# Four small moves in a one-core attention + MLP kernel: the q eviction of quad 1, the load of alpha, what delays the first casting transfers, and the PSUM tiles of one A@V

## The chip, the cores and the metric

The kernel runs on one core of a Trainium2 chip. The metric is the device time of one execution in microseconds; each version is run several times and its median is taken. A core has five engines that each work through their own list of instructions in order: TensorE (PE: matmuls, PEld: weight loads), VectorE (DVE), ScalarE (ACT), GpSimd (POOL) and SyncE (SP). They wait for each other through semaphores only. DMAs are issued from the lists of SP, ACT and POOL.

## The reference, cut to what matters

```python
def _attn_ref(q, k, v):                    # 8 batches, 12 heads, 448 positions, head size 64
    scores = scale * np.matmul(q, k.transpose(0, 1, 3, 2))
    attn = np.maximum(scores, 0.0) ** 2 / S
    return np.matmul(attn, v)

def _moe_ref(x, w_in, w_out, alpha):       # x: 3584 x 768, hidden size 2048
    h = x @ w_in
    g = np.maximum(h, 0.0) + alpha * np.minimum(h, 0.0)
    return g @ w_out
```

Attention without a softmax (relu, then squared) is followed by a two-layer MLP with a leaky relu whose slope alpha is given for each hidden unit. All inputs are float32; the kernel multiplies in bfloat16 and accumulates in float32.

## The kernel before, in words

**Tiling.** Four heads of one batch are a *quad*: two pairs (index r or s) of two heads (on the two halves of the 128 partitions). There are 3 quads in a batch (g = 0 to 2) and 24 in all. The 448 positions are 7 groups (j) of 64. For a unit (n, j), that is quad n and key group j, `scores` (L169) runs four 64x64 matmuls into a PSUM tile, then a relu writes it to SBUF as `rl`: "act" is one ACT instruction on 128x896 (L185), "both" one half on ACT (L163) and one on DVE (L165). `squares` (L188) multiplies two such units at a time by themselves on DVE (L196, 128x1792); its argument `keep` says how many finished units it may leave for later. `attnv` (L208) multiplies the seven squared units of a quad with v (28 matmuls, L223) and evicts the result, scaled, to `xT`. The MLP's first layer is `ffn1` (L248): 6 matmuls of 128x448 for each of the 16 blocks of 128 hidden units, over the six 128-row pieces km of the input (km // 2 is the quad g of the batch), then ACT writes the negative part (`neg`, L262) and DVE forms `gT` with beta = 1 - alpha (L263). The second layer is `ffn2` (L266).

**PSUM.** `sc_ps` (tag sc) has two buffers of two banks each, `mm_ps` (tag mm) four of one bank. A new tile in a pool waits for the readers of the tile that had the buffer before.

**Getting q, k and v in.** Of quad 0, q and k come as float32 on SP's queue (L357, L360: k in two pieces, groups 0 to 2 and 3 to 6) and are cast by ACT and DVE (L372, L373, L375, L378). Later quads of batches 0 and 1 come by DMAs that cast to bfloat16 on the way, issued by POOL (`load_bf16`, L93, and L367). PE transposes them to PSUM (`transpose`, L119, matmuls at L131), and DVE (L106) or ACT (L104) copies the result to `qT` and `kT`. From quad 6 on, other ways are used. The early casts live in `early_pool`, two buffers for each of q and k.

**Order.** The schedule is manual: each engine's list has its instructions in the order in which the program emits them. The start-up (L341 to L386) does quad 0's first units; the loop over n = 0 to 2 (L387 to L411) does the rest of batch 0's scores. Within it, at j = 3 the transposes and the eviction of k of quad n + 1 are emitted, at j = 4 those of q. After each unit, L398 calls `squares(keep=1)`; its condition `j != 4 or last or not 0` is always true:

```python
            elif j != 4 or last or not 0:
                squares(keep=1)
```

So at n = 0, j = 4 the square of units (0, 2) and (0, 3) stands in DVE's list ahead of the copy of quad 1's q. From the end of this loop on, MLP matmuls of one batch fill PE around the attention of the next.

**alpha.** It is 8 KB, loaded by ACT's queue first of all (L352). PE transposes it (L384) after the first scores, and DVE makes beta of it (L385). A one-column POOL copy from alpha into quad 1's k tile (L366) makes the first casting transfer (L367) wait until alpha has landed; the casts of quad 1's q, of v of quads 0 and 1 and so on follow it in POOL's list.

**The last A@V of batch 1.** `attnv(5)` (L471) takes one `sc_ps` tile for both halves, and one ACT instruction on 128x896 evicts it (L241). Around it stand `ffn1(1, 0)`, `ffn1(1, 1)` before, and `ffn1(1, 2)` behind, all with km = 0 to 3; then the matmuls with km = 4 and 5, which read what this eviction writes (L474, L475). `feed(7, "v")` (L472), a DVE cast, is emitted just after `attnv(5)`. With `apart=True`, which L422 uses for quad 2, an A@V takes two `sc_ps` tiles, and for later batches a list of two tiles is evicted by DVE (L238) and ACT (L239), a half each.

Of the kernel before, what the change touches and what calls it, by code (L numbers as in the profile page):

```python
# [11 lines left out]
BF16 = mybir.dt.bfloat16  # L12
# [8 lines left out]
NJ = 7  # L21
# [3 lines left out]
def kernel(  # L25
# [10 lines left out]
    nc = tc.nc  # L36
    B, H, S, D = q.shape
    d_model, d_ff = moe_w_in.shape
    assert H * D == d_model and S == PP * NJ and D == 64 and H % 4 == 0
    NG = H // 4  # L40
    n_pe = 2 * NG
    KM = d_model // 128
    KF = d_ff // 128
# [4 lines left out]
    def pool(name, bufs, **kw):  # L48
        return ctx.enter_context(tc.tile_pool(name=name, bufs=bufs, **kw))
# [6 lines left out]
    early_pool = pool("early", 2)  # L56
# [12 lines left out]
    alpha_sb = singles.tile([KF, 128], F32)  # L69
# [7 lines left out]
    raw, cast, qT, kT, vb = {}, {}, {}, {}, {}  # L77
    src = {"q": q, "k": k, "v": v}

    def flat(n, w):  # L80
        b, g = quads[n]
        return src[w][b, 4 * g:4 * g + 4].rearrange("(s hf) (pp j) d -> (hf pp) s (j d)", hf=2, j=NJ)

    def load(n, names="qkv", after=None):
        for w in names:
            t = raw_pool.tile([128, 2, NJ, D], F32, tag=w, name=f"{w}raw")
            raw[(n, w)] = t
            if after is not None:
                nc.gpsimd.tensor_copy(t[:, 0, 0, 0:1], after)
                after = None  # L90
            nc.sync.dma_start(out=t.rearrange("p s j d -> p s (j d)"), in_=flat(n, w))

    def load_bf16(n, names="kqv"):  # L93

        for w in names:
            if w == "v":
                t = vb[n] = v_pool.tile([128, 2, NJ, D], BF16, tag="v", name="vb")
            else:
                t = cast[(n, w)] = early_pool.tile([128, 2, NJ, D], BF16, tag=w, name=f"{w}e")
            nc.gpsimd.dma_start(out=t.rearrange("p s j d -> p s (j d)"), in_=flat(n, w))  # L100
# [7 lines left out]
    def to_bf16(n, w, eng):  # L108
        r = raw.pop((n, w))
        if w == "v":  # L110
            t = v_pool.tile([128, 2, NJ, D], BF16, tag="v", name="vb")
            vb[n] = t
            copy(eng, t, r)
        else:
            t = cast_pool.tile([128, NJ, 2, D], BF16, tag=w, name=f"{w}b")
            cast[(n, w)] = t
            copy(eng, t.rearrange("p j s d -> p s j d"), r)

    def transpose(n, w, js=range(NJ), eng=None):  # L119
        store = qT if w == "q" else kT  # L120
        if n not in store:
            store[n] = qkT_pool.tile([128, NJ, 2, PP], BF16, tag=w, name=f"{w}T")
        t, dst = cast[(n, w)], store[n]
        if n >= n_pe:
            nc.sync.dma_start_transpose(out=dst.rearrange("p j h c -> p j (h c)"),
                                        in_=t.rearrange("p j s d -> p (j s d)"))
            return
        ps = mm_ps.tile([128, NJ, 2 * PP], BF16, tag="mm", name="tps")
        for j in js:
            for s in range(2):  # L130
                nc.tensor.transpose(ps[64 * s:64 * s + 64, j], t[:, s, j], ident)  # L131
        lo, hi = js[0], js[-1] + 1
        copy(eng or nc.vector, dst[:, lo:hi].rearrange("p j h c -> p j (h c)"), ps[:, lo:hi])
# [74 lines left out]
    def attnv(n, js=range(NJ), space=sc_ps, apart=False):  # L208
        b, g = quads[n]
        if js[0] == 0:  # L210
            if space is mm_ps:
                av_ps[n] = [mm_ps.tile([128, 512], F32, tag="mm", name="avh") for _ in range(2)]
            elif apart:
                av_ps[n] = [sc_ps.tile([128, 2, 512], F32, tag="sc", name="av2")[:, 0] for _ in range(2)]
            else:
                av_ps[n] = sc_ps.tile([128, 2, 512], F32, tag="sc", name="av")
        ps = av_ps[n]
        half = ps if isinstance(ps, list) else [ps[:, r] for r in range(2)]
        for j in js:
            a = att.pop((n, j))  # L220
            for r in range(2):
                for s in range(2):
                    nc.tensor.matmul(half[r][64 * s:64 * s + 64, :S],  # L223
                                     vb[n][64 * r:64 * r + 64, s, j, :],
                                     a[64 * r:64 * r + 64, s],
                                     start=(j == 0), stop=(j == NJ - 1))
        if js[-1] != NJ - 1:
            return
        if g == 0:
            xT[b] = xT_pool.tile([128, NG, 2, S], BF16, tag="xT", name="xT")  # L230
        if b == 0:
            nc.scalar.activation(xT[b][:, g, 0], half[0][:, :S], ACTF.Copy, scale=out_scale)  # L232
            if g > 0:
                nc.vector.tensor_scalar(xT[b][:, g, 1], half[1][:, :S], out_scale, None, ALU.mult)
            else:
                nc.scalar.activation(xT[b][:, g, 1], half[1][:, :S], ACTF.Copy, scale=out_scale)
        elif isinstance(ps, list):
            nc.vector.tensor_scalar(xT[b][:, g, 0], half[0][:, :S], out_scale, None, ALU.mult)  # L238
            nc.scalar.activation(xT[b][:, g, 1], half[1][:, :S], ACTF.Copy, scale=out_scale)  # L239
        else:  # L240
            nc.scalar.activation(xT[b][:, g], ps[:, :, :S], ACTF.Copy, scale=out_scale)  # L241
# [69 lines left out]
    NQ = len(quads)  # L311
    def group(units, how="both"):

        def f():
            order = sorted(units, key=lambda u: u[1] == "av")
            for i, (n, j) in enumerate(order):
                if j == "av":
                    if (n, NJ - 1) not in att:
                        squares(single=nc.vector)
                    attnv(n)  # L320
                elif i == 0 and len(order) == 3:
                    scores(n, j, how, mm_ps)
                else:
                    scores(n, j)
            squares()
            for n, j in order:
                if n < n_pe:
                    continue
                if j == 0:
                    if n + 2 < NQ:  # L330
                        load(n + 2)
                    if n + 1 < NQ:
                        transpose(n + 1, "k")
                        transpose(n + 1, "q")
                if j == 4 and n > 2 * NG and n + 2 < NQ:
                    for w in "kqv":
                        to_bf16(n + 2, w, nc.gpsimd)
        return f


# [8 lines left out]
        for _ in range(count):  # L349
            nc.tensor.matmul(ps[:, 0, :256], warm_w, warm_x, start=True, stop=True)  # L350

    nc.scalar.dma_start(out=alpha_sb, in_=moe_alpha.rearrange("(kf p) -> kf p", p=128))  # L352
    for w in "qk":
        raw[(0, w)] = raw_pool.tile([128, 2, NJ, D], F32, tag=w, name=f"{w}raw")
        cast[(0, w)] = early_pool.tile([128, 2, NJ, D], BF16, tag=w, name=f"{w}e")
# [2 lines left out]
    for js in (first, rest):  # L358
        lo, hi = js[0], js[-1] + 1
        nc.sync.dma_start(out=raw[(0, "k")][:, :, lo:hi].rearrange("p s j d -> p s (j d)"),  # L360
                          in_=flat(0, "k")[:, :, lo * D:hi * D])
    make_identity(nc, ident)
    make_identity(nc, ident_f)

    cast[(1, "k")] = early_pool.tile([128, 2, NJ, D], BF16, tag="k", name="ke")
    nc.gpsimd.tensor_copy(cast[(1, "k")][:KF, 0, 0, 0:1], alpha_sb[:, 0:1])  # L366
    nc.gpsimd.dma_start(out=cast[(1, "k")].rearrange("p s j d -> p s (j d)"), in_=flat(1, "k"))  # L367
    load_bf16(1, "q")
    load_bf16(0, "v")
    load_bf16(1, "v")  # L370
    warm(15)
# [15 lines left out]
    for n in range(NG):  # L387
        last = n == NG - 1
        for j in range(NJ):
            if n == 0 and j < 3:  # L390
                continue
            if j == 2 or j == (4 if last else 5):
                scores(n, j, "both", mm_ps)
            else:
                scores(n, j, "act")
            if j == 6 and last:
                squares()
            elif j != 4 or last or not 0:  # L398
                squares(keep=1)
            if j == 3 and n > 0:  # L400
                attnv(n - 1, space=mm_ps)
            if j == 3 and not last:
                transpose(n + 1, "k")
            if j == 4 and not last:
                transpose(n + 1, "q")
                squares(keep=1)

            if last and j > 4:
                ffn1(0, j - 5, range(0, 4))
            if last and j == 6:  # L410
                ffn1(0, 2, range(0, 4))  # L411
        if n == 0:
            load_bf16(2)
            load_w_in(0, 512)
            load_w_in(512, 1024)
            load_w_in(1024, 2048)
            load_bf16(3)
# [41 lines left out]
    f = [fn for _, fn in steps(0, "in")]  # L459
# [8 lines left out]

    ffn1(1, 0, range(0, 4))
    ffn1(1, 1, range(0, 4))  # L470
    attnv(5)  # L471
    feed(7, "v")()  # L472
    ffn1(1, 2, range(0, 4))
    for ff in range(3):  # L474
# [107 lines left out]
```

## Time and profile before

| what | value |
|---|---|
| median of 4 runs | 391.56 us |
| lowest and highest run | 391.09 and 393.16 us |
| the profiled execution's own time | 391.09 us |
| its span, first to last instruction | 389.3 us |
| time around the span | 1.8 us |
| granted TensorE clock | 1.000 |
| busy: PE, DVE, ACT, POOL | 379.2, 252.6, 215.6, 74.0 us |

Times inside the profile count from the start of the span. A group line names the source line, the engine, the operation, and output <- input; in the timeline the first two numbers are the start and the length in us of one or several (xN) merged instructions, and the square bracket tells how long the engine had been idle before and what ended that. The chain of waits is the sequence of work that ended last, followed back from the end. Durations of matmuls overlap: in a dense stretch 96 matmuls of 128x448 take 18.16 us, 0.19 each, while the row of a single one says 0.35.

### The profile page before, as it was taken

The page shows a single profiled execution, that of the slowest core. Times are in us where ns is not written, and L with a number is a line of the kernel's source. Part 1 is how long each engine was busy: PE and PEld are TensorE (multiplying, and loading weights), DVE is VectorE, ACT ScalarE, POOL GpSimd, SP SyncE. Part 2 cuts the span into 40 slices and gives each one's busy share as a digit, 9 for nine tenths or more (in the row PEclk, how much of TensorE's full clock was granted, in tenths as well). Part 3 has the DMA queues.
Part 4 walks back from the last instruction along what each step waited for, and adds up shares of the span by engine and source line. Part 5 has one row for each costly group of instructions (what it writes and reads, how often), then busy time and mean ns, then how long its engine had stood idle before and what let it go on. Part 6 is the DMA issues. An engine that isn't in the chain of part 4 may idle for free.

```text
span 389.3 us, 7871 instructions
## 1 busy us (share of the span) xinstructions
PE 379.2 (97%) x3210; PEld 215.1 (55%) x3210; DVE 252.6 (65%) x335; ACT 215.6 (55%) x361; POOL 74.0 (19%) x88
## 2 busy tenths in 40 slices
PE   7699999999999999999999999999999999999996
PEld 4345556445665456645665455654566545655564
DVE  3976887687687767766675666777676376726411
ACT  5964768564566656664573645756565366624200
POOL 6654000052241113201231012311030000000000
PEclk9999999999999999999999999999999999999999
DMA  7999998995994619735494355947153220130033
GB/s 161 187 209 204 205 207 289 259 252 123 262 264 166 128 64 242 220 67 162 100 262 142 68 163 100 271 132 186 18 91 88 69 47 2 42 81 2 0 83 81
DMA packets 64755, 55.43 MB, mean 142 GB/s; under 512 B 35776, under 2 KB 60496, under 8 KB 64720
## 3 DMA queue, kind: packets, MB, share of 16 engines
q1 hardware_dynamic: 53472, 44.77, 45.2%
q0 software_dynamic: 10976, 9.96, 16.1%
q8 instruction: 25, 0.41, 0.4%
q10 hardware_dynamic: 272, 0.21, 0.2%
q14 instruction: 10, 0.08, 0.1%
HBM read 45.62 MB, written 11.01 MB: 145 GB/s over the span
## 4 chain that ended last, share of the span: by engine, by line
PE 93%; ACT 3%; DVE 1%; DMA 1%; issue 1%; ACTq 0%
PE hps L255 37%; PE ops L271 37%; PE avh L223 7%; PE sc L156 6%; PE sch L156 3%; ACT rl L185 2%; PE ops L294 1%; PE av L223 1%; PE tps L131 1%; DMA qraw<-in_q_dram 1%; DVE at L196 0%; ACT xT L232 0%; ACT xT L241 0%; ACT rl L163 0%; DVE gT L263 0%
## 5 line engine op out<-in xcount | busy, mean ns | idle before, releaser
L255 PE MATMUL hps<-xT,w_in_sb 128*128 128x448 bf16 x768 | 149.3, 353 | 0.8 <-ACT xT L232 0.4
L271 PE MATMUL ops<-w_out_sb,gT 128*128 128x384 bf16 x864 | 145.8, 326 | 0.1
L263 DVE SCALAR_TENSOR_TENSOR gT<-neg,beta_sb,hps 128x448 bf16<-128x448 f32 x128 | 85.6, 679 | 60.8 <-ACT neg L262 60.0
L271 PEld LDWEIGHTS <-gT 128*128 128x128 bf16 x864 | 83.5, 98 | 61.1 <-issue 7.9
L255 PEld LDWEIGHTS <-w_in_sb 128*128 128x128 bf16 x768 | 74.0, 98 | 72.8 <-issue 5.9
L262 ACT ACTIVATE neg<-hps 128x448 f32<-128x448 f32 x128 | 69.2, 546 | 63.7 <-PE hps L255 62.9
L185 ACT ACTIVATE rl<-sc 128x896 bf16<-128x896 f32 x87 | 77.4, 927 | 44.0 <-PE sc L156 44.0
L196 DVE TENSOR_TENSOR at<-rl 128x1792 bf16<-128x1792 bf16 x80 | 86.2, 1121 | 2.1 <-ACT rl L185 0.9
L106 DVE COPY osb<-ops 128x384 f32<-128x384 f32 x30 | 16.7, 557 | 45.7 <-PE ops L271 45.7
L163 ACT ACTIVATE rl<-sch 128x448 bf16<-128x448 f32 x81 | 41.7, 552 | 4.6 <-PE sch L156 4.6
L106 POOL CAST kb<-kraw 128x896 bf16<-128x896 f32 x16 | 18.7, 1166 | 114.1 <-DMA kT<-kb 56.7
L156 PE MATMUL sc<-qT,kT 64*64 64x448 bf16 x456 | 35.9, 355 | 4.1 <-ACT rl L185 1.4
L223 PE MATMUL avh<-at,vb 64*64 64x448 bf16 x588 | 34.2, 350 | 0.0
L156 PEld LDWEIGHTS <-kT 64*64 64x64 bf16 x672 | 21.9, 106 | 20.3 <-issue 12.8
L104 ACT COPY osb<-ops 128x384 f32<-128x384 f32 x24 | 11.4, 475 | 36.0 <-PE ops L271 36.0
L223 PEld LDWEIGHTS <-vb 64*64 64x64 bf16 x672 | 25.6, 106 | 9.3 <-issue 4.5
L183 DVE TENSOR_SCALAR rl<-sc 128x896 bf16<-128x896 f32 x27 | 29.4, 1090 | 0.6 <-PE sc L156 0.6
L106 POOL CAST vb<-vraw 128x896 bf16<-128x896 f32 x16 | 15.9, 992 | 36.3 <-PE avh L223 36.0
L106 POOL CAST qb<-qraw 128x896 bf16<-128x896 f32 x16 | 16.6, 1035 | 32.4 <-DMA qT<-qb 32.4
L156 PE MATMUL sch<-qT,kT 64*64 64x448 bf16 x216 | 22.5, 355 | 0.0
L165 DVE TENSOR_SCALAR rl<-sch 128x448 bf16<-128x448 f32 x27 | 16.8, 623 | 2.6 <-ACT xT L239 0.8
L238 DVE TENSOR_SCALAR xT<-avh 128x448 bf16<-128x448 f32 x19 | 11.9, 626 | 7.7 <-PE avh L223 7.7
(55 smaller groups left out, 97.7 us busy)
## 6 DMA issues: line engine op xcount, KB each, us to landing
out_dram<-osb SPq DMA_DIRECT2D x54, 192.0 KB, 2.8
qraw<-in_q_dram SPq DMA_DIRECT2D x19, 448.0 KB, 5.4
kraw<-in_k_dram SPq DMA_DIRECT2D x18, 448.0 KB, 4.4
vraw<-in_v_dram SPq DMA_DIRECT2D x18, 448.0 KB, 6.0
w_out_sb<-in_moe_w_out_dram POOLq DMA_DIRECT2D x2, 1536.0 KB, 20.1
w_in_sb<-in_moe_w_in_dram POOLq DMA_DIRECT2D x8, 192.0 KB, 8.5
w_in_sb<-in_moe_w_in_dram POOLq DMA_DIRECT2D x4, 384.0 KB, 10.0
vb<-in_v_dram POOLq DMA_DIRECT2D x6, 224.0 KB, 9.4
```

Source lines behind the costliest of these rows:

```text
L106: eng.tensor_copy(o, i)
L156: nc.tensor.matmul(half[r][64 * c:64 * c + 64, :S], kT[n][64 * r:64 * r + 64, j, c, :], qT[n][64 * r:64 * r + 64, :, c, :], start=True, st ...
L163: nc.scalar.activation(rl[:, r], half[r][:, :S], ACTF.Relu)
L165: nc.vector.tensor_scalar(rl[:, r], half[r][:, :S], 0.0, None, ALU.max)
L183: nc.vector.tensor_scalar(rl, ps[:, :, :S], 0.0, None, ALU.max)
L185: nc.scalar.activation(rl, ps[:, :, :S], ACTF.Relu)
L196: nc.vector.tensor_tensor(a, t, t, ALU.mult)
L223: nc.tensor.matmul(half[r][64 * s:64 * s + 64, :S], vb[n][64 * r:64 * r + 64, s, j, :], a[64 * r:64 * r + 64, s], start=(j == 0), stop=(j ...
L255: nc.tensor.matmul(ps, w_in_sb[:, km // 2, km % 2, bass.ts(ff, 128)], xT[b][:, km // 2, km % 2, :], start=(km == 0), stop=(km == KM - 1))
L262: nc.scalar.activation(neg, ps, ACTF.Relu, scale=-1.0)
L263: nc.vector.scalar_tensor_tensor(gT[b // 2][:, ff, (b % 2) * S:(b % 2) * S + S], neg, beta_sb[:, ff:ff + 1], ps, ALU.mult, ALU.add)
L271: nc.tensor.matmul(ps, gT[sb][:, ff, bass.ts(c, 128)], w_out_sb[:, ff, bass.ts(hf, 384)], start=(ff == 0), stop=(ff == KF - 1))
```

## The change

- **q of quad 1.** At n = 0, j = 4 the call of `squares` ahead of `transpose(1, "q")` is left out; the call behind it (unchanged) emits the same square. In DVE's list the copy of q of quad 1 and the square of units (0, 2), (0, 3) change places. Nothing else in the loop differs.
- **alpha.** Its DMA goes from the head of ACT's list to SP's, behind the three loads of quad 0.
- **Casting transfers.** POOL's one-column copy that waited for alpha is gone. Instead POOL fills quad 1's q tile and then its k tile with zeros (two memsets of 128x896 bfloat16), and the two transfers into them follow, k first as before.
- **A@V of quad 5.** It takes two `sc_ps` tiles and is evicted in two halves, by DVE (L238, 128x448) and ACT (L239, 128x448), where one ACT instruction did all of it. In DVE's list the new eviction stands ahead of the cast of v of quad 7.
- A stretch of `group` that no call reaches is removed; line numbers below it fall by up to 12.

```diff
@@ group
             squares()
-            for n, j in order:
-                if n < n_pe:
-                    continue
...
@@ start-up
-    nc.scalar.dma_start(out=alpha_sb, in_=moe_alpha.rearrange("(kf p) -> kf p", p=128))
     for w in "qk":
         raw[(0, w)] = raw_pool.tile([128, 2, NJ, D], F32, tag=w, name=f"{w}raw")
...
+    nc.sync.dma_start(out=alpha_sb, in_=moe_alpha.rearrange("(kf p) -> kf p", p=128))
     make_identity(nc, ident)
     make_identity(nc, ident_f)
 
-    cast[(1, "k")] = early_pool.tile([128, 2, NJ, D], BF16, tag="k", name="ke")
-    nc.gpsimd.tensor_copy(cast[(1, "k")][:KF, 0, 0, 0:1], alpha_sb[:, 0:1])
-    nc.gpsimd.dma_start(out=cast[(1, "k")].rearrange("p s j d -> p s (j d)"), in_=flat(1, "k"))
-    load_bf16(1, "q")
+    for w in "qk":
+        cast[(1, w)] = early_pool.tile([128, 2, NJ, D], BF16, tag=w, name=f"{w}e")
+        nc.gpsimd.memset(cast[(1, w)], 0.0)
+    for w in "kq":
+        nc.gpsimd.dma_start(out=cast[(1, w)].rearrange("p s j d -> p s (j d)"), in_=flat(1, w))
     load_bf16(0, "v")
@@ loop over batch 0
             if j == 6 and last:
                 squares()
-            elif j != 4 or last or not 0:
+            elif n > 0 or j != 4:
                 squares(keep=1)
@@ batch 1
-    attnv(5)
+    attnv(5, apart=True)
     feed(7, "v")()
```

More of the change, by code (lines that the diff above doesn't have):

```diff
@@ L325, in f @@
             squares()
-            for n, j in order:
-                if n < n_pe:
-                    continue
[L329 to L337, printed above, removed]
         return f
```

## The prediction, made before the changed kernel was run

> **What bounds the kernel now.** I read the chain of waits first, then the timeline where the chain leaves PE, then each engine's own timeline there, then the landings of the POOL transfers.
>
> The page's chain by engine and by line:
>
> ```profile
> PE 93%; ACT 3%; DVE 1%; DMA 1%; issue 1%; ACTq 0%
> ```
>
> 93% is PE, in an unbroken run of matmuls but for two places: the first 22 us and one eviction. Only there can the change win time; anywhere else it can only lose. The chain of the first 30 us, and of 68 to 78 us:
>
> ```profile
> 0.74 3.51 DMA qraw<-in_q_dram
> ...
> 10.14 1.00 DVE at L196
> 11.14 0.55 DVE qT L106
> ...
> 11.73 0.41 PE sc L156 x4
> ...
> 20.69 0.69 ACT xT L232
> ...
> 21.42 0.92 PE hps L255 x4
> ```
> ```profile
> 70.80 1.48 PE av L223 x28
> 72.28 0.02 issue
> 72.30 0.93 ACT xT L241
> 73.23 0.04 issue
> 73.27 3.00 PE hps L255 x15
> ```
>
> The first fence shows the square of (0, 2), (0, 3) and the q copy in series ahead of quad 1's scores; the second, one ACT eviction that PE waits for. PE and DVE in their own timelines of the start:
>
> ```profile
> 9.31 0.58 PE L131 MATMUL tps<-ident,qe 128*64 128x128 bf16 x14
> 11.73 0.57 PE L156 MATMUL sc<-qT,kT 64*64 64x448 bf16 x8 [1.34 <-DVE qT L106]
> 13.32 0.38 PE L223 MATMUL avh<-at,vb 64*64 64x448 bf16 x4
> ```
> ```profile
> 9.52 0.62 DVE L106 COPY kT<-tps 128x896 bf16<-128x896 bf16 x1
> 10.06 1.08 DVE L196 TENSOR_TENSOR at<-rl 128x1792 bf16<-128x1792 bf16 x1
> 11.06 0.62 DVE L106 COPY qT<-tps 128x896 bf16<-128x896 bf16 x1
> 11.59 0.61 DVE L165 TENSOR_SCALAR rl<-sch 128x448 bf16<-128x448 f32 x1
> 12.31 2.09 DVE L196 TENSOR_TENSOR at<-rl 128x1792 bf16<-128x1792 bf16 x2
> ...
> 21.18 0.62 DVE L234 TENSOR_SCALAR xT<-avh 128x448 bf16<-128x448 f32 x1
> ```
>
> What decides my forecast: from 8.52 to 24.87 DVE has no gap over 0.1 us. It is full, though the chain names ACT. PE's 1.34 us of idleness is thus not simply to be had.
>
> POOL's start, and the landing views of its first two transfers (last number: us from issue to landing):
>
> ```profile
> 1.43 0.19 POOL masks.py:199 TENSOR_SCALAR_AFFINE_SELECT ident_f<-ident_f 16x16 f32<-16x16 f32 x1
> 3.46 0.18 POOL L366 CAST ke<-alpha_sb 16x1 bf16<-16x1 f32 x1 [1.84 <-DMA alpha_sb<-in_moe_alpha_dram]
> 3.95 0.86 POOL L367 DMA_DIRECT2D ke<-in_k_dram  x1 [0.31 <-POOL ke L366]
> ```
> ```profile
> ke<-in_k_dram POOLq DMA_DIRECT2D x1, 224.0 KB, 4.1
> ```
> ```profile
> qe<-in_q_dram POOLq DMA_DIRECT2D x1, 224.0 KB, 4.4
> ```
>
> k of quad 1 lands at 3.95 + 4.1 = 8.05 and PE transposes it at 8.48; q lands at 4.81 + 4.4 = 9.21 and is transposed at 9.31. Margins: 0.43 and 0.10 us.
>
> **The change part by part.**
>
> *q ahead of the square.* The q transposes end at 9.31 + 0.58 = 9.89 and DVE is done with the k copy at 10.14, so the q copy takes the square's place and ends at about 10.68 instead of 11.68. The square then ends at 11.68, and DVE's next instruction (the relu half at 11.59) starts when it did: same two instructions, same sum. Behind the q copy: quad 1's first scores need the buffer of (0, 4), free at 10.54, so they go at 10.73, and ACT is next: its relu of (0, 6) began at 10.81, and relus follow each other 0.87 apart, so that of (1, 0) starts at 11.68, not 12.16. ACT gains 0.48. Three places take it back. A@V of quad 0 could begin about 0.48 earlier than 13.32, but its last group (6 x 0.195 us in, at 14.49) needs the second square of the pair at 12.31, which ends at 14.40: gain 0.09 at most. ACT then waits for this A@V and keeps 0.18 (15.00 to about 14.82). Quad 2's scores wait for DVE's q copy, which ends at 17.20 as before, but a relu there waits longer for ACT than for them, so 0.18 survives. The MLP's first four matmuls begin at 21.42 - 0.18 = 21.24; the fourth, at 21.42 + 3 x 0.19 = 21.99 before, reads what L234 writes on DVE until 21.80: it can go at 21.84. Gain 0.15 us. From there PE is dense to 72 us and carries it. The bounds are 0 (DVE only) and 0.48 (ACT's full lead); I take 0.15, since it is DVE's rows that I can follow to their end.
>
> *alpha on SP.* ACT loses one issue of 0.46 us ahead of an activation-table load that ends at 2.52, while its first data come at 4.28: nothing. SP's two k issues end at 2.22, so alpha is issued there; SP issues nothing more until 55.68. With the slowest landing of quad 0's loads (3.7 us) it lands near 5.9 and is read by PE at 7.36: covered by 1.4 us. If that cover were gone, the units (0, 3) and on would wait behind the alpha transpose in PE's list. q may land a few hundredths earlier without alpha beside it; between 0 and 0.1, I take 0.
>
> *Two memsets for one wait.* POOL is free at 1.62. A memset of 128x896 isn't in the trace. Below: 128x1 took 0.10 and 128x128 0.205 us, 0.8 ns an element, so 0.82 us. Above: POOL's cast of 128x896 has a minimum and a median of 0.937 and a maximum of 1.9 us. I take 0.9, near the cast's median, as DVE is idle until 4.28 and nothing disturbs POOL. Two end at 3.45; with the 0.31 between POOL's copy and the issue before, the k transfer is issued at 3.76 instead of 3.95, 0.2 us earlier (bounds: 0.35 earlier to 1.8 later). All that follows on this queue lands as much earlier, since the queue is backed up until 58 us. Early or on time is worth nothing, PE's transposes stand behind other work at 8.17 and 8.99. Do the transfers collide with quad 0's loads? In the 1 us slices of the first 40 us those moved 20, 157, 387 and 352 KB until 5.0, and the slice to 6.0 has 29 KB: 0.2 us earlier stays in this hole, and k's second piece is cast only at 6.05. Cost 0. The margin that shrinks: q copied first stands in front of the square, so a late q now stops DVE. It starts to cost when q lands more than about 0.14 us later than before.
>
> [...]
>
> *A@V of quad 5.* One ACT instruction of 0.917 us (72.30 to 73.22) becomes 0.544 on ACT (row L239) beside 0.626 on DVE (row L238). DVE's last work ended at 70.79, and the v cast moves behind to about 73.5; its raw buffer is wanted by a load that SP issues at 75.31, its product much later. km = 4 can go at 72.30 + 0.63 + 0.04 = 72.97 instead of 73.27; PE's four matmuls before it end their issue at 72.18 + 4 x 0.19 = 72.94. Gain 0.30. km = 5 at 73.16 needs ACT, done at 72.85. The second `sc_ps` buffer was last read by a relu that ended at 68.06. Both bounds: 0 and 0.33, the whole stall. PE is dense from here to the end.
>
> **Sum**: -0.15 - 0.30 = -0.45 us. The profiled execution took 391.09 (span 389.3 + 1.8), so 390.64; it is the fastest of four, and against their median of 391.56 the same gain gives 391.1.
>
> **The rivals.**
>
> 1. *ACT, not DVE, sets the start.* The chain speaks for it (ACT from 12.16 to 21.38), DVE's gapless rows against. The start gains 0.48, in all 0.78: 390.8.
> 2. *The casting transfers come too late (slower).* Place: PE's transposes of quad 1 at 8.48 and 9.31, and the q copy behind them, which DVE now meets before the square. If a memset costs POOL's slowest cast, 1.9, the issue is at 1.65 + 3.8 + 0.31 = 5.76, q lands 1.8 later, 1.67 of it past the margin; in all +1.2: 392.8. It decides from about 0.6 us of delay on, a memset of 1.29 us. Against it: all undisturbed rows of POOL.
> 3. *The split eviction wins nothing*, because a half on DVE starts late or PE's next wait takes its place: then only 0.15 is left: 391.4. Against it: 19 such pairs elsewhere in the trace, 0.544 and 0.626 us.
>
> **How the numbers follow.** Forecast 0.53, rival 1 0.2, rival 2 0.12, rival 3 0.1, 0.05 for something I don't see. All named cases lie within 0.5% (1.96 us) of the median, which is about what a measurement of this kernel can tell from no change: 0.91 there. Beyond it, slower 0.05 (rival 2 with still slower memsets, or the unseen) and faster 0.04. The median of four moves inside a spread of 2 us by itself, so the range goes beyond rival 1 below, 390.0, and includes most of rival 2 above, 392.4.
>
> **What would show it.** Right: DVE's order k copy, q copy, square, with the relu half still near 11.6; PE's scores of quad 1 near 10.7; the first MLP matmuls near 21.2; two memsets of about 0.9 ending near 3.5; the 15-matmul group near 72.8 (73.27 less 0.30 and 0.15). Wrong: PE waiting for the k or q cast before 10 us, a DVE gap ahead of the q copy, or memsets above 1.3 us.

## The result and the profile after

The changed kernel takes 390.97 us (median of 43 executions, 390.58 to 391.95); the kernel before, run beside it, 391.52 us (70 executions, 391.03 to 393.83). The ratio is 0.9984, 95% interval 0.9979 to 0.9990: 0.63 us faster (0.39 to 0.82; the medians differ by 0.55), well inside the 0.5% that was named as the bound of "the same". The prediction, 391.1 (390.0 to 392.4), holds the time. Its sum was -0.45 us. The profiled execution of the changed kernel took 390.93 us with a span of 389.1; that of before had 391.09 and 389.3.

That the total came out does not mean that the terms did. The parts have to be looked at one by one, and the profile after allows that. First the page's chain by engine, then the two stretches of the chain of waits that the prediction quoted (start in us, duration, what):

```profile
PE 94%; ACT 2%; DMA 1%; DVE 1%; POOL 1%; issue 0%; POOLq 0%; DVEq 0%
```
```profile
4.32 5.29 DMA qe<-in_q_dram
...
9.65 0.60 PE tps L131 x14
...
10.28 0.04 DVE qT L106
...
10.82 1.08 DVE at L196
```
```profile
70.90 1.45 PE av L223 x28
72.35 3.71 PE hps L255 x19
```

The last fence is the simple part: the 0.93 us of ACT and the two issues that stood between A@V and the MLP are gone, and 19 matmuls follow without a break. The fence above it is new. Before, the chain entered through the load of quad 0's q (`qraw`, issued at 0.74). Now it enters through `qe`, the casting transfer of quad 1's q. That is the margin of 0.10 us that the prediction had noted, and it is used up. PE and DVE in their own timelines show where (start, duration, engine, line, operation; in brackets the idle time ahead and what ended it):

```profile
8.63 0.58 PE L131 MATMUL tps<-ident,ke 128*64 128x128 bf16 x14 [0.26 <-DMA ke<-in_k_dram]
9.14 0.38 PE L156 MATMUL sc<-qT,kT 64*64 64x448 bf16 x4
9.65 0.58 PE L131 MATMUL tps<-ident,qe 128*64 128x128 bf16 x14
...
10.96 0.38 PE L156 MATMUL sc<-qT,kT 64*64 64x448 bf16 x4 [0.22 <-DVE qT L106]
```
```profile
8.33 1.09 DVE L196 TENSOR_TENSOR at<-rl 128x1792 bf16<-128x1792 bf16 x1 [0.31 <-ACT rl L185]
9.34 0.62 DVE L106 COPY kT<-tps 128x896 bf16<-128x896 bf16 x1
10.28 0.62 DVE L106 COPY qT<-tps 128x896 bf16<-128x896 bf16 x1 [0.33 <-PE tps L131]
10.82 1.08 DVE L196 TENSOR_TENSOR at<-rl 128x1792 bf16<-128x1792 bf16 x1
11.82 0.62 DVE L165 TENSOR_SCALAR rl<-sch 128x448 bf16<-128x448 f32 x1
...
21.41 0.62 DVE L234 TENSOR_SCALAR xT<-avh 128x448 bf16<-128x448 f32 x1
```

The order is as foreseen: k copy, q copy, square, relu half. PE's 1.34 us of waiting ahead of quad 1's scores is down to 0.22. But there is a gap of 0.33 us ahead of the q copy, which the prediction listed as a sign of error, and L234, which gates the MLP's fourth matmul, starts at 21.41 instead of 21.18. POOL's start, and the landings (last number: us from issue to landing):

```profile
1.56 0.84 POOL L355 MEMSET qe<- 128x896 bf16 x1
2.34 0.83 POOL L355 MEMSET ke<- 128x896 bf16 x1
3.49 0.84 POOL L357 DMA_DIRECT2D ke<-in_k_dram  x1 [0.31 <-POOL ke L355]
4.32 0.72 POOL L357 DMA_DIRECT2D qe<-in_q_dram  x1
```
```profile
ke<-in_k_dram POOLq DMA_DIRECT2D x1, 224.0 KB, 5.0
qe<-in_q_dram POOLq DMA_DIRECT2D x1, 224.0 KB, 5.3
```

k was issued at 3.49, 0.46 us earlier than before, and landed at 8.49, 0.44 later than before (8.05). q was issued 0.49 earlier and landed at 9.62, 0.41 later.

To compare runs, the chain is cut at three fixed points: S, the first 128x1792 square on DVE; the start of A@V of quad 5 (70 to 73 us); the first matmul of unit (6, 0). Behind the last point the profiles of this study have 312.8 to 313.1 us left (390.8 - 77.8 in one, 388.6 - 75.6 in another). S in the timeline of before:

```profile
8.52 1.09 DVE L196 TENSOR_TENSOR at<-rl 128x1792 bf16<-128x1792 bf16 x1 [0.32 <-ACT rl L185]
```

| profile | S | S to A@V 5 | A@V 5 to (6, 0) | span |
|---|---|---|---|---|
| before | 8.52 | 62.28 | 5.47 | 389.3 |
| after | 8.33 | 62.57 | 5.16 | 389.1 |

So the start up to S gained 0.19, the stretch behind it lost 0.29, and the eviction gained 0.31. The prediction had 0, -0.15 and -0.30. One profile is one execution; which of this is the change, and which is the execution, the experiments tell.

One thing about single executions has to be known for the medians below. The mean granted clock of an execution is not always 1.0. In the three groups of experiments, 26 of 99 executions of the kernel before had a mean of 0.996 or less, with a median of 392.92 us; the other 73 had 391.38. "At full clock" means 0.998 or more. The two do not coincide altogether: six of those 73 took 392.85 us or more.

### The profile page after: what moved, and what is told of

Its sections match the earlier page's. It is cut to its first block, busy times and chain, and to the rows that moved or that the text cites. A ratio compares the mean times of both kernels' runs of the same rounds, so it can differ in the third digit from the quotient of the medians.

```text
span 389.1 us, 7873 instructions
## 1 busy us (share of the span) xinstructions
PE 379.6 (98%) x3210; PEld 214.9 (55%) x3210; DVE 252.5 (65%) x336; ACT 215.4 (55%) x361; POOL 74.9 (19%) x89
## 4 chain that ended last, share of the span: by engine, by line
PE 94%; ACT 2%; DMA 1%; DVE 1%; POOL 1%; issue 0%; POOLq 0%; DVEq 0%
PE hps L255 38%; PE ops L271 37%; PE avh L223 7%; PE sc L156 6%; PE sch L156 3%; DMA qe<-in_q_dram 1%; PE ops L294 1%; PE av L223 1%; PE tps L131 1%; ACT rl L185 1%; DVE at L196 1%; ACT xT L232 0%; POOL ke L357 0%; POOL ke L355 0%; POOL qe L355 0%
## 5 line engine op out<-in xcount | busy, mean ns | idle before, releaser
L106 POOL CAST vb<-vraw 128x896 bf16<-128x896 f32 x16 | 16.7, 1046 | 37.1 <-PE avh L223 36.8
L238 DVE TENSOR_SCALAR xT<-avh 128x448 bf16<-128x448 f32 x19 | 11.9, 625 | 7.7 <-PE avh L223 7.7
```

Of the source, the lines that this page charges most:

```text
L106: eng.tensor_copy(o, i)
```

## Experiments

Each part of the change was made alone, undone alone, or made larger. The three groups (e1 to e4, e5 to e8, f1 to f4) ran on three chips, each beside the kernel before, whose executions have medians of 391.58 (e1 to e4) and 391.49 (both others); times of different groups are thus times of different chips. Unless noted there are 12 executions of each. Their medians resolve about 0.7 us, the cut chain of a profile some 0.1, so the medians are given and the verdicts rest on the profiles.

**The split eviction alone (e1).**

```diff
-    attnv(5)
+    attnv(5, apart=True)
```

> Before, with only the A@V of quad 5 in two tiles. My theory (PE waits for one long eviction, then is dense to the end): 0.30 us faster, the 15 matmuls of the first MLP layer begin 0.3 us after the A@V without a gap. Rival (the next wait takes its place): 0.0.

Measured: 391.35 against 391.58 us, ratio 0.9995 (0.9977 to 1.0013); span 389.2. The chain of waits of e1 at the eviction:

```profile
71.03 1.45 PE av L223 x28
72.47 3.71 PE hps L255 x19
```

From A@V 5 to (6, 0) it takes 5.16 us, as in the changed kernel and 0.31 less than before; S to A@V 5 is 62.30, unchanged. That is the term of 0.30, alone. S itself was at 8.73, so that little of it is left in the span: the start varies from one execution to the next by about as much as this part is worth.

**q ahead of the square, alone (e2).**

```diff
-            elif j != 4 or last or not 0:
+            elif n > 0 or j != 4:
                 squares(keep=1)
```

> Before, with only the q copy of quad 1 ahead of the square. My theory (DVE's sum of work sets the start): 0.15 us faster (0 to 0.2), the fourth matmul of the MLP gated by DVE's L234 near 21.8. Rival (ACT sets it): 0.48 us faster, the MLP's first matmul near 20.9.

Measured: 391.80 against 391.58, ratio 1.0009 (0.9990 to 1.0029); span 389.7. S to A@V 5 took 62.35: no gain. PE's timeline of e2 shows the reason six microseconds behind the place that was changed:

```profile
16.20 0.58 PE L131 MATMUL tps<-ident,qe 128*64 128x128 bf16 x14 [0.18 <-DMA qe<-in_q_dram]
```

This is quad 2's q. The same row of before:

```profile
15.60 0.58 PE L131 MATMUL tps<-ident,qe 128*64 128x128 bf16 x14
```

There the transfer had landed at 15.49, 6.97 us behind S; in e2 it landed at 16.15, 7.28 behind S (issue and time to landing, 8.69 + 6.8 and 9.05 + 7.1). PE is no earlier at this place (it begins quad 2's k transposes 6.26 us behind S, 6.25 before), but it waits for q, the transposes come 7.33 behind S instead of 7.08, and the lead that ACT had won ends there.

**alpha on SP and the two memsets, alone (e3).**

```diff
-    nc.scalar.dma_start(out=alpha_sb, in_=moe_alpha.rearrange("(kf p) -> kf p", p=128))
...
+    nc.sync.dma_start(out=alpha_sb, in_=moe_alpha.rearrange("(kf p) -> kf p", p=128))
...
-    nc.gpsimd.tensor_copy(cast[(1, "k")][:KF, 0, 0, 0:1], alpha_sb[:, 0:1])
...
+        nc.gpsimd.memset(cast[(1, w)], 0.0)
```

> Before, with only alpha on SP and the two memsets for the wait on alpha. Theory A (the casts issued earlier land later, as in the profile of the changed kernel, where k and q landed 0.4 us later although issued 0.46 earlier): PE waits for the k and q casts at about 8.6 and 9.65, the square covers most of it: 0 to 0.2 us slower. Theory B (landings scatter from one execution to the next, and q of quad 0 lands 0.1 to 0.15 earlier without alpha beside it): 0 to 0.15 us faster.

Measured: 391.22 against 391.58, ratio 0.9997 (0.9977 to 1.0016); span 389.5. DVE begins to cast quad 0's q at 3.89 instead of 4.28, so the loads alone bring that data in earlier. S is nevertheless at 8.61: in this execution the 14 transposes of q that follow took 314 ns each, against 224 before (more on that in the last section). k of quad 1 was issued at 3.48 and landed at 8.18, q at 4.32 and 9.32, 0.11 later than before.

**The changed kernel again (e4).** The same program as the changed kernel, run beside the parts.

> The changed kernel once more, for a second profile. Theory A: k and q of quad 1 land again near 8.5 and 9.6. Theory B: they land elsewhere, by more than 0.2 us. Time: 0.4 to 0.8 us faster than before.

Measured: 391.08 against 391.58, ratio 0.9977 (0.9959 to 0.9995); span 388.6. S at 8.15, S to A@V 5 in 62.29, then 5.16. A second execution of one program thus gives -0.37, +0.01, -0.31 where the first gave -0.19, +0.29, -0.31. Only the last number is firm. q of quad 1 was issued at 4.31 here and 4.32 there; it landed after 4.8 us here and 5.3 there.

**alpha back on ACT, the rest as changed (e5).**

```diff
+    nc.scalar.dma_start(out=alpha_sb, in_=moe_alpha.rearrange("(kf p) -> kf p", p=128))
...
-    nc.sync.dma_start(out=alpha_sb, in_=moe_alpha.rearrange("(kf p) -> kf p", p=128))
```

> The changed kernel with alpha's load back at the head of ACT's list; the memsets stay. Theory L (alpha beside it delays q of quad 0: it landed at 3.87, 3.93 and 4.11 in the three profiles with alpha on SP, and at 4.20, 4.25 and 4.30 in the three with alpha on ACT): q of quad 0 lands near 4.25, and the time is up to 0.28 us above the changed kernel's. Rival (scatter): q lands anywhere between 3.9 and 4.3, no difference in time.

Measured: 391.57 against 391.49, ratio 0.9997 (0.9981 to 1.0012); at full clock 391.53, against 391.00 for e4 on another chip; span 389.2. The first cast on DVE, in the timelines of before, e4 and e5:

```profile
4.28 0.40 DVE L372 CAST qe<-qraw 128x448 bf16<-128x448 f32 x1 [3.20 <-DMA qraw<-in_q_dram]
```

```profile
3.93 0.58 DVE L361 CAST qe<-qraw 128x448 bf16<-128x448 f32 x1 [2.86 <-DMA qraw<-in_q_dram]
```
```profile
4.27 0.40 DVE L361 CAST qe<-qraw 128x448 bf16<-128x448 f32 x1 [3.19 <-DMA qraw<-in_q_dram]
```

All kernels of this study divide by that line. With alpha on SP the cast starts at 3.89 to 4.13 (seven profiles, mean 4.01), with alpha on ACT at 4.22 to 4.39 (seven profiles, mean 4.31). They do not overlap: 0.30 us. The prediction had 0 to 0.1 and took 0. e5 also shows what the q order is worth when nothing is late: its casting transfers landed in time for PE (k at 3.48 + 4.7 us, transposed at 8.89, q at 4.31 + 5.1, transposed at 9.72), and S to A@V 5 took 62.15, 0.13 less than before.

**More alpha (e8).** If the bytes of alpha are what delays q, three more of them delay it more.

```diff
     nc.scalar.dma_start(out=alpha_sb, in_=moe_alpha.rearrange("(kf p) -> kf p", p=128))
+    alpha_x0 = singles.tile([KF, 128], F32)
+    nc.scalar.dma_start(out=alpha_x0, in_=moe_alpha.rearrange("(kf p) -> kf p", p=128))
...
```

> Before, with three further loads of alpha (to tiles that nobody reads) behind the first on ACT's list. Theory L: each small load that shares the DMA engines with q of quad 0 costs it the same, so q lands 0.3 to 0.8 us later than 4.25 and the kernel is that much slower. Rival: q lands within 0.1 of 4.25, as its 448 KB dwarf 8 KB.

Measured (10 executions): 391.48 against 391.49, ratio 1.0001 (0.9983 to 1.0019); span 389.5. DVE's first cast:

```profile
4.33 0.42 DVE L378 CAST qe<-qraw 128x448 bf16<-128x448 f32 x1 [3.25 <-DMA qraw<-in_q_dram]
```

4.33, no later than with one alpha (4.31). An explanation by the amount of data falls. So does one by ACT's activation-table load, which e8 moved from 1.24 to 2.63 us. What is left is that alpha was issued at 0.74, in the same moment as q; whether the issue or something in the transfer engines delays q was not told apart.

**No memsets (e6).** The transfers are issued as soon as POOL is free.

```diff
     for w in "qk":
         cast[(1, w)] = early_pool.tile([128, 2, NJ, D], BF16, tag=w, name=f"{w}e")
-        nc.gpsimd.memset(cast[(1, w)], 0.0)
```

> The changed kernel without its two memsets (nothing delays the casting transfers: k issued near 1.9 instead of 3.5; what the memsets wrote is overwritten anyway). Theory A (they take turns with the loads of quad 0): q and k of quad 0 land later by 0.3 to 1 us and the start with them; 0.2 to 0.8 us slower than the changed kernel. Theory B (the loads of quad 0 keep their time): k and q of quad 1 land 1 us earlier or more, PE's waits for them at 8.6 and 9.65 go, q first then wins its 0.15: 0.15 to 0.4 faster than the changed kernel.

Measured: 392.73 against 391.49, ratio 1.0024 (1.0000 to 1.0047); span 390.1. k of quad 1 is issued at 1.63. Quad 0's q is not touched (cast at 4.09), but the second piece of its k, 256 KB on SP, lands after 6.3 us instead of 3.7. DVE's timeline of e6:

```profile
8.07 0.43 DVE L366 CAST ke<-kraw 128x512 bf16<-128x512 f32 x1 [2.12 <-DMA kraw<-in_k_dram]
```

The same cast before:

```profile
6.05 0.45 DVE L378 CAST ke<-kraw 128x512 bf16<-128x512 f32 x1
```

The memsets are thus what keeps the casting transfers out of quad 0's loads; S moves to 9.43 without them. Theory A holds for the second piece of k and not for q, and the span is 1.0 to 1.5 us above the two profiles of the changed kernel (389.1 and 388.6), more than its 0.8.

**Each memset twice (e7).** The rival of the late transfers, forced.

```diff
         nc.gpsimd.memset(cast[(1, w)], 0.0)
+        nc.gpsimd.memset(cast[(1, w)], 0.0)
```

> The changed kernel with each memset done twice (k issued near 5.05 instead of 3.49). Issue theory: q of quad 1 lands 1.5 later than 9.15 to 9.6, PE and then DVE wait for it, 1.2 to 1.5 us slower than the changed kernel, some 0.7 slower than before. Drain theory (landing is set by when the DMA engines are done with quad 0): it lands 0.5 to 0.9 later, 0.4 to 0.8 us slower than the changed kernel.

Measured (6 executions): 393.93 against 391.49, ratio 1.0057 (1.0036 to 1.0079), and the span of the profiled execution 390.8. PE's timeline of e7:

```profile
9.75 0.58 PE L131 MATMUL tps<-ident,ke 128*64 128x128 bf16 x14 [1.26 <-DMA ke<-in_k_dram]
```

k is issued at 5.52, q lands at 10.76, S to A@V 5 takes 64.21. That is 1.9 more than before and, with the 0.31 of the eviction and an S close to before's, 1.5 us in the span. Against the two profiles of the changed kernel it is 1.7 to 2.2, with q landing 1.1 to 1.7 later: the issue theory, with some more on top. Part of that is quad 2's q, for which PE waits again (0.44 us, at 17.65). The median is further up than the span since 4 of the 6 executions had the lower clock.

**q order undone (f1).** The changed kernel with the old condition.

```diff
-            elif n > 0 or j != 4:
+            elif j != 4 or last or not 0:
                 squares(keep=1)
```

> The changed kernel with the order of before in DVE's list (square of (0, 2), (0, 3), then the q copy of quad 1). Theory D (DVE's sum sets the start, and the square ahead of the q copy covers a late q): the MLP's first matmul 12.90 us after the first square, as in before; 0.0 to 0.15 us faster than the changed kernel in an execution of full clock. Theory G (the changed order fills PE's gap of 1.3 us in front of quad 1's scores, and that keeps the granted clock up): the gap is back, and executions with a mean granted clock of 0.996 or less, 20 of 64 of the kernel before and 1 of 56 of the changed one, come back to a fifth or more of the runs; median up by 0.2 or more.

Measured: 391.18 against 391.49, ratio 0.9988 (0.9967 to 1.0010); span 388.6. This is the clearest reading of what the order does. q of quad 1 is late here too, for PE:

```profile
9.37 0.58 PE L131 MATMUL tps<-ident,qe 128*64 128x128 bf16 x14 [0.24 <-DMA qe<-in_q_dram]
...
11.38 0.70 PE L156 MATMUL sc<-qT,kT 64*64 64x448 bf16 x8 [0.93 <-DVE qT L106]
```

but DVE does not notice:

```profile
9.18 0.62 DVE L106 COPY kT<-tps 128x896 bf16<-128x896 bf16 x1
9.71 1.08 DVE L196 TENSOR_TENSOR at<-rl 128x1792 bf16<-128x1792 bf16 x1
10.71 0.62 DVE L106 COPY qT<-tps 128x896 bf16<-128x896 bf16 x1
...
20.84 0.62 DVE L234 TENSOR_SCALAR xT<-avh 128x448 bf16<-128x448 f32 x1
```

The square covers the wait. L234 starts 12.67 us behind S, as in the kernel before (12.66), and S to A@V 5 takes 62.29. At full clock f1 is the fastest kernel of the study, 390.66 (7 executions) against 390.98 of the changed kernel; but 5 of its 12 executions had the lower clock, against 1 of 56 of the changed kernel (44 of the result's and 12 of e4's), and so its median is not better.

**Eviction undone (f2).** The changed kernel with `attnv(5)`.

> The changed kernel without the split eviction of quad 5's A@V. My theory: 0.30 us slower than the changed kernel, its A@V followed by a gap until 0.97 us later. Rival (the next wait takes its place, as the time of the split alone, 0.1 faster among executions of full clock, could be read): 0.1 or less.

Measured: 391.15 against 391.49, ratio 0.9987 (0.9973 to 1.0000); span 389.6. The chain of waits of f2 has the stall back:

```profile
71.11 1.48 PE av L223 x28
72.59 0.02 issue
72.61 0.93 ACT xT L241
```

A@V 5 to (6, 0) takes 5.47 again. By the executions at full clock this part is worth 0.13 (391.11 against 390.98, mostly on other chips), by the profiles 0.31; the former is too small a sample to contradict the latter. k and q of quad 2 were late in this execution (PE waits 0.29 us for k, at 15.14), and S to A@V 5 took 62.59.

**Loads undone (f3).** The kernel before with the q order and the split eviction.

> The changed kernel with alpha on ACT and the wait on alpha instead of the memsets (q first and the split eviction alone). Theory L (alpha beside q of quad 0 costs the start 0.2 to 0.3): q of quad 0 lands near 4.25, 0.2 to 0.5 us slower than the changed kernel. Theory G alone: as fast as the changed kernel, with at most 1 of 12 executions at a clock of 0.996 or less. If both loads and order are needed for the clock: 3 or more of 12.

Measured: 391.24 against 391.49, ratio 0.9993 (0.9978 to 1.0008); span 389.0. DVE's timeline of f3:

```profile
9.66 0.62 DVE L106 COPY kT<-tps 128x896 bf16<-128x896 bf16 x1
10.19 0.62 DVE L106 COPY qT<-tps 128x896 bf16<-128x896 bf16 x1
10.73 1.08 DVE L196 TENSOR_TENSOR at<-rl 128x1792 bf16<-128x1792 bf16 x1
```

Here q is on time, the copies stand shoulder to shoulder, and the changed order shows what it can do: the first MLP matmul is 12.74 us behind S instead of 12.90, S to A@V 5 62.15 instead of 62.28. L234 is 12.67 behind S, as ever. At full clock f3 takes 391.20 us, 0.22 more than the changed kernel's 390.98 on other chips, which fits theory L without proving it, and 1 of its 12 executions had the lower clock.

**PE's gap filled with work that counts for nothing (f4).** The kernel before with eight of its warm-up matmuls put into PE's wait at 10.4 to 11.7 us.

```diff
+            if n == 0 and j == 6:
+                warm(8)
             if last and j > 4:
```

> Before, with eight matmuls on zeros (128x256, results unused) put into PE's idle 1.34 us ahead of quad 1's scores; they take an extra score tile, so those scores start at most 0.1 later. Theory G (idleness of PE in the start lowers the granted clock): at most 1 of 12 executions at a mean clock of 0.996 or less where the kernel before has about 4 of 12; median 0.1 slower to 0.2 faster. Rival (the clock has nothing to do with this gap): 3 or more of 12.

Measured: 391.79 against 391.49, ratio 0.9993 (0.9977 to 1.0009); span 389.5. PE's timeline of f4:

```profile
10.70 1.03 PE L350 MATMUL warm<-warm_x,warm_w 128*128 128x256 bf16 x8 [0.19 <-ACT rl L185]
11.95 0.57 PE L156 MATMUL sc<-qT,kT 64*64 64x448 bf16 x8 [0.21 <-ACT rl L185]
```

The chain is that of before (S to A@V 5 62.38, then 5.47). The 12 executions all had the full clock, where 6 of 35 of the kernel before had not on the same chip (26 of 99 on all three); 12 are few to tell 0 from that. Its time at full clock is 0.4 above before's (391.79 against 391.38), which the profile doesn't explain.

The chains of all profiles, for reference:

| run | S | S to A@V 5 | A@V 5 to (6, 0) | span |
|---|---|---|---|---|
| e1 | 8.73 | 62.30 | 5.16 | 389.2 |
| e2 | 8.87 | 62.35 | 5.47 | 389.7 |
| e3 | 8.61 | 62.38 | 5.46 | 389.5 |
| e4 | 8.15 | 62.29 | 5.16 | 388.6 |
| e5 | 8.92 | 62.15 | 5.16 | 389.2 |
| e6 | 9.43 | 62.44 | 5.16 | 390.1 |
| e7 | 8.46 | 64.21 | 5.16 | 390.8 |
| e8 | 8.90 | 62.29 | 5.47 | 389.5 |
| f1 | 8.17 | 62.29 | 5.16 | 388.6 |
| f2 | 8.52 | 62.59 | 5.47 | 389.6 |
| f3 | 8.65 | 62.15 | 5.16 | 389.0 |
| f4 | 8.63 | 62.38 | 5.47 | 389.5 |

## Why the prediction came out right, point by point

*A@V of quad 5, -0.30.* Right in size and place. Every profile with the split has 5.16 us from A@V 5 to (6, 0), every one without it 5.46 or 5.47: 0.31 us. Rival 3 (the split wins nothing) is refuted by e1 and f2.

*q ahead of the square, -0.15.* Half right. The argument "DVE is full" held: L234 starts 12.66 or 12.67 us behind S in the kernel before and in e1, e2, e3, e5, e8, f1, f3 and f4, in either order of the copies. Rival 1, by which ACT's lead of 0.48 would come through, is refuted. The gain of 0.13 to 0.16 us is there in e5 and f3. But it is there only when the casting transfers land in time, and they did not in after, e4, e2 and f2: S to A@V 5 was +0.29, +0.01, +0.07 and +0.31 against before. Two steps failed. One is "All that follows on this queue lands as much earlier": q of quad 1 was issued at 4.31 or 4.32 in six profiles with the memsets once (after, e3, e4, e5, f1, f2) and at 4.55 to 4.81 in six of the old order of loads (before, e1, e2, e8, f3, f4), 0.34 earlier in the mean, but the mean landing is 9.32 against 9.43, and it spreads over 0.5 us in the one group and 0.8 in the other: in after and e4, the same program, k landed at 8.49 and 7.58, q at 9.62 and 9.11. With S 0.3 earlier, the margin of 0.10 us was gone. The other is "so 0.18 survives" at quad 2, where I let a relu decide and did not look at the landing of its q, 0.1 us ahead of its transposes; PE's wait in e2 at 16.20 stands there.

*alpha on SP, 0.* The mis-sized term: 0.30 us at DVE's first cast in fourteen profiles. "q may land a few hundredths earlier" saw the effect and took a tenth of it. e8 shows that the amount that is loaded beside it isn't what counts. It reaches S, the first 128x1792 square, whose mean is 8.75 in the seven profiles with alpha on ACT and 8.37 in six with alpha on SP (e6 is left out, its S waits for another load). The speed of the early transposes also moves S (last section), but in each of its two classes the difference stays: 8.60 against 8.22, and 8.86 against 8.53.

*Two memsets, 0.9 us each.* They took 0.83 to 0.84 us, at the lower bound, and started 0.78 apart; k went 0.46 earlier, not 0.2. That costs nothing by itself, and it does not collide with quad 0's loads, as foreseen (the second piece of its k is cast at 5.91 us, before at 6.05). e6 shows that the hole that they aim at is real.

*The issue beside DVE's cast.* In before the first k issue (3.95 to 4.81) lies around DVE's cast (4.28 to 4.68) and took 0.86 us, against 0.72 of later ones. The difference is not DVE's doing: in e6 this issue took 0.84 at 1.63 us, when DVE was idle until 4.09, and the q issue took 0.72 beside the cast in after (4.32) and e4 (4.31). On DVE's side, the first cast took 0.58 to 0.62 us where it began some 0.4 us before the end of the k issue (e3, e4, f1), and 0.39 to 0.46 in the other eleven, before with its 0.40 among them. No delay of q comes from it; q's late landings have another cause, which stays open.

*Rival 2, late casts.* Its mechanism is real: PE and then DVE stop for a late cast, and e7 pays 1.5 us in the span for about 1.5 us of delay of q (10.76 against 9.21), where the rival's working (delay less 0.14, less 0.45 of gains) gives 1.0. The change meets it only in tenths of a microsecond.

*The sum.* -0.31 for the eviction, -0.30 to -0.37 for alpha, between 0 and +0.3 for the order with late casts: from -0.7 to -0.3. Two profiles of the changed kernel lie at -0.2 and -0.7, and the time at full clock fell by 0.40 over all groups (390.98 against 391.38) and by 0.44 on the chip of e4 (391.00 against 391.44). That the forecast of -0.45 came out is luck in its terms: the gain I had not seen paid for one that was lost. The rest of the 0.63 us goes with something that the prediction didn't have at all. Of the 70 executions of before that ran beside the changed kernel, 9 lie above 392.5 us, apart from all the others; without them the means differ by 0.41 instead of 0.62, and the medians by 0.52 instead of 0.55. The changed kernel had none such there. The clock of these 70 is not on record; in the groups of experiments 26 of 99 executions of before had the lower clock, and of the changed kernel's, there and in the result's run, 1 of 56.

The signs: relu half at 11.82 instead of 11.6, scores at 10.96 instead of 10.7, the MLP's first matmul at 21.49 instead of 21.2, each late by the gap ahead of the q copy, a sign of error that was listed, as was PE's wait for the k cast (0.26 us, at 8.63). The 15-matmul group began 15 x 0.2 us ahead of (6, 0) at 76.06, so near 73.06, where 72.8 was foretold.

## What to carry to other kernels

A margin of 0.1 us on a transfer is no margin: its landing spread over 0.5 us between executions of one program, so moving an in-order engine's copy ahead of a square that used to cover it trades a sure cover for a gain only when the data is early. Read the landing margins of every later stage that the same lead will reach, not just those of the stage that is edited. And where parts are worth 0.3 us in 390, cut the chain at fixed points in several profiles: the parts show there, while medians of 12 executions only show their sum.

## What the runs showed of the hardware

*The clock.* The mean granted clock of single executions lies at 0.998 and above, or at 0.996 and below, mostly near 0.996 and 0.991, with some in between. In each of the 14 traces its record has two entries: full rate (1.0) from a moment between 3.8 and 6.8 us on, and half rate (0.5) from 387.9 us or later, at least 2 us behind PE's last matmul. The stretch ahead of the first entry does not enter the mean, and half rate at the end is all that makes the 0.998 and 0.999 of four of these profiles (e1, e2, e3, e8). Executions of before at 0.996 or less are 1.54 us slower in the median (392.92 against 391.38). In the kernels with PE's wait at 10 to 12 us (1.34 us in before, e1 and e3, 1.15 in e8, 0.93 in f1), 40 of 145 executions were so; in those where it is 0.22 or 0.33 (after, e2, e4, e5, f2, f3), 7 of 104; in f4, where matmuls without use fill it, 0 of 12; in e6 and e7, where PE waits as long a little earlier (1.35 and 1.26 us), 7 of 12 and 4 of 6. Chip by chip it is less even: beside e1 to e4 before had 13 of 35, but e1 and e3 with the wait had 5 of 24 and e2 and e4 without it 4 of 24. The counts thus point to an idle PE early in the kernel as what costs the clock in a share of the executions, and don't prove it. No profile caught an execution with a mean of 0.996 or less, so that it happens in this very wait is inferred, not seen.

The entry of full rate lasts 382.29 us in five of the traces (e1, e2, e3, e5, e8) and 385.71 in the other nine. An estimate from these lengths and the recorded means: over 385.71 us a mean of 0.996 is 1.54 us of full rate lost, and the 19 executions of before at 0.996 are 1.53 us slower; a mean of 0.991 is 3.47 us lost, but the 7 at 0.991 and 0.989 are only 2.31 us slower.

*TensorE's first microseconds.* The transposes of quad 0's q took 222 to 224 ns each in seven profiles (before, after, e4, e6, f1, f3, f4) and 291 to 314 ns in seven (e1, e2, e3, e5, e7, e8, f2). The same groups, in the window of 4.5 to 7 us, of before and of e2 (behind the bar: busy us, mean ns of one, idle us before):

```profile
L131 PE MATMUL tps<-ident,qe 128*64 128x128 bf16 x14 | 0.7, 224 | 0.2 <-DVE qe L372 0.2
```
```profile
L131 PE MATMUL tps<-ident,qe 128*64 128x128 bf16 x14 | 1.1, 314 | 0.2 <-DVE qe L372 0.2
```

The record of the clock in the traces goes with it: full rate is entered at 3.81 to 4.72 us in the first seven and at 5.20 to 6.76 in the others, when these transposes have begun. From DVE's first cast to S it takes 4.20 to 4.27 us in the first (without e6) and 4.41 to 4.72 in the others. It goes with the execution, not with the kernel: up to 70 us e1 is the kernel before (5.58 against 4.72), and f2 the changed kernel (5.40 against 4.30 in after and 4.25 in e4). S is later by 0.25 us in the mean with alpha on ACT (8.86 against 8.60) and by 0.31 with alpha on SP (8.53 against 8.22), as much as any part of this change is worth.

*Loads at the same moment.* An 8 KB load that ACT issued together with the first 448 KB load on SP made the latter 0.30 us later at its reader; three more behind it added nothing (means of the first cast 4.31 and 4.01, seven profiles each; 4.33 in e8). The cause stays open.
